# A hand-laid order of five instruction lists, laid out anew: Sinkhorn attention and a two-layer feed-forward block on one core

## The chip, the cores and the metric

The kernel runs on one NeuronCore of a Trainium2 chip. The core has a matrix engine (PE, TensorE), three engines for element-wise work (DVE, ACT and POOL), and a sequencer engine (SP) that here only issues transfers. Each engine works through its own list of instructions, strictly in order, and waits on semaphores for the others. Transfers are issued by POOL (loads from device memory that convert f32 to bf16) and by SP (transposing copies inside the on-chip memory, and the stores of the result).

The metric is the device time of one execution in microseconds: the median over several runs.

## What is computed

Four batches (B) with eight heads (H), 768 positions, 64 channels. The sequence is cut into eight blocks of 96. A learned 8x8 matrix per batch and head is made doubly stochastic by five rounds of Sinkhorn normalisation, and mixes the blocks of k and of v. Each block of q then attends to its own mixed block. The result, 3072 tokens of 512 channels, goes through a feed-forward block with a learned slope for negative values.

```python
for _ in range(5):
    P = np.exp(P - np.max(P, axis=-1, keepdims=True))
    P = P / (np.sum(P, axis=-1, keepdims=True) + 1e-09)
    P = P / (np.sum(P, axis=-2, keepdims=True) + 1e-09)
k_sorted = np.einsum('bhij,bhjcd->bhicd', P, k_b)
v_sorted = np.einsum('bhij,bhjcd->bhicd', P, v_b)
scores = scale * np.matmul(q_b, k_sb.transpose(0, 1, 2, 4, 3))
attn = softmax(scores)
x = np.matmul(attn, v_sb)          # then (B, S, H*D) -> 3072 x 512
h = x @ w_in                       # 512 -> 2048
g = np.maximum(h, 0.0) + alpha * np.minimum(h, 0.0)
out = g @ w_out                    # 2048 -> 512
```

## The kernel before

The kernel first builds a graph of 1190 steps. A step is a small function that issues one or some instructions, with the engines that may run it, the tiles it reads and writes, and so the steps it depends on (`_Graph.add`). A step that may run on two or three engines carries no fixed one (`EITHER`, `ANY`, `SMALL`).

The order is written out by hand in the constant `SEQ`: a list of step numbers. `arrange` walks through it and appends each step to the list of its engine. A letter behind a number (`p`, `a`, `d`) puts the step on POOL, ACT or DVE; without one it goes to the first engine that it may use. An entry such as `i15Y` isn't a step of the graph but 15 filler products: PE multiplies the identity with itself into the PSUM bank of that letter, and nobody reads the result (line 1047). `emit` then works out, for these five lists, the semaphore waits that are left. So the order of the steps on each engine, the engine of the free steps, and the number and place of the fillers follow from `SEQ` alone.

The work in stages, for one batch or for the whole:

- **Start.** PE runs a burst of 208 tiny products and then fillers, while q, k and v of batch 0 are loaded and the Sinkhorn rounds go back and forth between DVE and ACT. The result `Pb` is spread over the partitions by PE (step 79), and DVE makes the mixing matrix of it.
- **Preparation of a batch.** `prep_q` transposes q (steps 81, 83, 85, 87 for batch 0); `prep_k` and `prep_v` mix the blocks on PE, and ACT, DVE or POOL copy the result into KT and VS. For batches 1 to 3, `conv_k` and `conv_v` first spread k and v into sparse tiles (KSz, VDz), mostly on POOL, and q is loaded head by head (QN, eight loads per batch) and turned by six transposing copies that SP issues (`turn_q`). Each of these six reads all eight heads.
- **Attention of block g** (0 to 31). Scores on PE (line 756 for batches 1 to 3), row maxima on DVE (nf, line 765), Exp on ACT (Esb, line 793), a transposing copy by SP (ET, line 798), product with V on PE (line 813), reciprocal and scaling (rec, xq), and a transposition into xT, by PE or by SP. Blocks of batch 0 take a way without the transposing copies.
- **Feed-forward.** `ffn1` makes 128 hidden channels for two or four blocks of tokens (line 875), ACT and DVE apply the slope (lines 885 and 889), and `ffn2` sums over the hidden channels for 128 tokens in four parts (line 915); a copy and a store follow. These two carry most of the products and are laid between the attention steps.

The steps that are named below:

| Steps | What they are |
|---|---|
| 4, 5, 6 | loads of q, k, v of batch 0 |
| 126 to 129 | loads of the four parts of w_in; the hidden channels of the first half need 126 and 127 |
| 130, 131 | loads of the two halves of w_out; the first two parts of `ffn2` need 130, the last two 131 |
| 134; 143, 144 | loads of k, and of the two halves of v, of batch 1 |
| 135 to 142 | loads of the eight heads of q of batch 1 |
| 173 to 178 | the six transposing copies of q of batch 1 |
| 365, 366; 367 | loads of the two halves of v, and of k, of batch 2 |
| 44 | the first Exp of the Sinkhorn rounds |
| 39, 40, 9 | copies of the identity on ACT: selk, sel0 and identb |
| 151, 153, 162 | scaling of block 0, and the copies into xT of blocks 0 and 1 |
| 188 | the first `ffn1` |
| 252 to 255 | the four parts of the first `ffn2` |
| 382, 385, 386 | scores of block 8 (the first of batch 1), its transposing copy, its product with V |

Of the kernel before, what the change touches and what calls it, by code (L numbers as in the profile page):

```python
# [38 lines left out]
232 206 183 230 184 207 192 193 185d 198 209 142 199 186 i1Y 231 237 210 141 194 195 221 208 131 187 213 200  # L39
211 212 222 244 214 201 223 215 216 248 245 224 249 202d 246 247 203 204d 250 251 217 225 258 218 236 226 262  # L40
263 219 220 234 241 235 227d 266 267 259 260 173 228 229 252 238 276 268 239 253 264 242 269 305 172 288d 170
174 240 280 261 279 286 243 270 315 265 289 290 277 278 271 287 293 294 306 307 272d 273 308 275 291 274 281
292 297 295 342 282d 298 283 309 284 296 301 302 285 316 343 317 310 299 344 300 328 311d 303 304 312 314 313d
320 326 332 32 321d 345 346 327 169p 333 324 329 347 325 353 348d 254 171p 349 334 335 175 354 255 256 350d
323 367 318 395 330 382 331 396 319d 392 336 351 393 383 384 397 394 419 416 420 322 352d 355 356 358d 31 365
398 399 337 366 357 338 408 421 409 359 257 425 417 400 418 426 422 339 428 360d 361 427 423 424 411 449 410
385 340 368 446 429 362 363 439 450 451 455 430 364d 447 448 369 176 458 459 414 443 456 415 386 387 388d 412
452 453 370 454 440 389 401 460 371 438 390d 402 476 488 457 479 413 403 404d 489 405 372 512 177 469 431 406d
432 477 178 441 461 480 444 478 482 442 481 485 433 434d 490 524 491 373 483 472 435 378 377 486 374 436 487
513 380 445 462 375 484 509 463 510 464d 470 379 471 506 507 381 511 465 466d 508 525 514 376 521 522 523 518  # L50
519 520 515 516d 526 527 492 517 474 545 475d 542 168 554 560 391 493 543 546 544 547 468 500 501 494d 555 548
473 561 549 550 502 437 495 496d 562 407 503d 551 552 556 499 577 553 563 578 579 498 504 505 533 528 529 557
558 589 530d 535 534 538 539 571 572 590 583 584 580 341 531 581 625 626 537 536 569 582 586 591 540 587 585
622 570d 541 573 574 575 532 600 576 627 588 623 631 598 624 599 564 632 559 628 629 565 601 634 566d 567 635
602 592 630 603 633 568d 637 636 655 638 639 608 604 605 593 594 595d 610 649 650 640 652 596 653 656 657 609
597 641 642 651 654 664 665 666 661 662 663 606 667 607 658 611 659 687 688 612 668 613 643 684 696 685 660
669 689 686 697 690 691 676 677 682 711 467 680 702 693 694 703 704 683d 695 678 698 692 699 679 713 714 644
645 497 700 670 705 722 723 731 732 810 712 719 720 751 681 733 734 717 817 744 752 646d 812 715 721 724 671
672 725 745 816 718 766 673d 728 767 742 753 726 727 647 729 730 674 706 748 701 757 707 768 618 769 743d 754
708d 758 759 749 750 801 802 755 756 716 746 763 764 747 735 736 760 737d 761 803 765 740 709 762 741 621 789  # L60
777 790 783 784 619 776 786 787 778d 813 785 779 788 836 837 791 792 780 793 775 781 738 804 795 796 782d 811
798 799 797 838 615 814 815d 620 830 770 614 617 818 819 844 845 800 616 771 821 772d 864 831 846 848 874 839
820 648 822 824 823 773 827 805 806 825 794 849 826 832 833 828 807d 829 808 847 872 852 875 865 675 855 873d
834 853 835 850 883 851 854 866 840 841 867 710 876 842d 843 774 877 884 856 857 858 878 879 885 886 898 899
887 859 861 860 912 913 862 880 863 868 869 870d 900 889 924 944 881 882 890 892 891 893 895 925 945 896 894
914 906 926 907 897 908 909 950 910 911 871 946 901 951 927 918 919 920 921 922 923 952 902 903 904d 915 739
932 933 934 935 936 947 948 928 953 970 937 938 939 905 941 942 916d 981 917 982 971 972 943 961 940 958 809
959 973 996 929 1010 930d 931 954 962 997 998 983 960 964 965 963 967 968 1022 955 956d 966 984 969 957 949
# [1021 lines left out]
```

## Time and profile before

| What | us |
|---|---|
| Median of three runs | 235.51 (234.73 to 236.08) |
| The profiled execution, its own time | 235.32 |
| Its span, from the first to the last instruction | 233.6 |
| PE busy in the span | 225.4 |
| DVE, ACT, POOL busy | 167.6, 156.0, 102.7 |

The profile is that of one execution. The span leaves out what lies before the first and behind the last instruction, 1.7 us here. In the lines that follow, L875 is line 875 of the kernel; PE is the matrix engine's products and PEld its weight loads, which overlap them. A timeline line gives the start, the length, the engine, the line, the operation and what it writes and reads; in brackets stands how long the engine was idle before it, and what ended that. Products overlap, so the length of a line with several of them is the time from the first start to the last end. A stretch's line gives its length, the busy time of each engine with the number of its instructions, and behind them the granted clock of PE, the share of the transfer engines and the GB/s.

### The profile page before, as it was taken

Reading aid. Unit: us, or ns where it says so; the run is one execution under the profiler, and the core shown is the slowest. Engines: PE = TensorE matmul, PEld = TensorE weight load, DVE = VectorE, ACT = ScalarE, POOL = GpSimd, SP = SyncE. Lnnn points to the kernel's source line nnn. Section 1 sums busy time; section 2 is a strip of 40 time slices with the busy share of each in tenths; the row PEclk is TensorE's granted clock in tenths of the full one; section 3 lists DMA queues with packets and bytes.
Section 4 is the critical chain, followed back from the end, with each engine's and each line's share of the span. In section 5 each row is a group of like instructions: output and inputs, shape, how many; then the busy total and the mean of one; then the engine's idle time right before and its main releaser. Section 6 shows DMA issues by size and latency. Waiting matters only on the chain.

```text
span 233.6 us, 6277 instructions
## 1 busy us (share of the span) xinstructions
PE 225.4 (96%) x2528; PEld 140.4 (60%) x2556; DVE 167.6 (72%) x339; ACT 156.0 (67%) x417; POOL 102.7 (44%) x149
## 2 busy tenths in 40 slices
PE   6989999999999999999999999999999999999995
PEld 4356588795666666665566565555555555555653
DVE  5769799999878788586689668467787677544541
ACT  4187666989889678778888677766676674333431
POOL 7999139849049994863969953000000000000000
PEclk9999999999999999999999999999999999999999
DMA  5999999996996899869939997944643523410203
GB/s 66 220 206 204 218 200 185 186 182 99 218 189 106 115 152 174 196 102 225 192 63 164 137 103 164 154 90 79 130 107 74 112 51 109 124 45 0 94 0 135
DMA packets 73389, 31.36 MB, mean 134 GB/s; under 512 B 64512, under 2 KB 68368, under 8 KB 73360
## 3 DMA queue, kind: packets, MB, share of 16 engines
q0 software_dynamic: 24816, 13.63, 43.5%
q1 hardware_dynamic: 48544, 17.33, 37.2%
q8 instruction: 20, 0.33, 0.6%
q14 instruction: 9, 0.07, 0.1%
HBM read 27.28 MB, written 6.29 MB: 144 GB/s over the span
## 4 chain that ended last, share of the span: by engine, by line
PE 86%; DMA 4%; POOL 4%; DVE 3%; issue 2%; ACT 1%; POOLq 0%
PE psH L875 33%; PE psYP L915 28%; PE psYP L1047 4%; DMA VST<-in_v_dram 4%; PE psS L915 4%; PE psO L813 3%; PE psS L756 3%; POOL VDz L401 2%; PE psYP L668 2%; PE psYP L709 2%; PE psS L771 1%; PE psO L848 1%; DVE hT L401 1%; PE psS L781 1%; PE psO L915 1%
## 5 line engine op out<-in xcount | busy, mean ns | idle before, releaser
L889 DVE SCALAR_TENSOR_TENSOR hT<-t,omaT,psH 128x384 bf16<-128x384 f32 (+1 forms) x140 | 76.5, 568 | 37.4 <-ACT t L885 36.5
L875 PE MATMUL psH<-xT,w_in_bf 128*128 128x384 bf16 (+1 forms) x560 | 96.7, 310 | 0.6 <-DVE hT L889 0.6
L885 ACT ACTIVATE t<-psH 128x384 f32<-128x384 f32 x126 | 60.9, 493 | 44.5 <-PE psH L875 41.6
L915 PE MATMUL psYP<-w_out_bf,hT 128*128 128x512 bf16 x310 | 79.2, 379 | 1.4
L875 PEld LDWEIGHTS psH<-xT,w_in_bf 128*128 128x128 bf16 x560 | 50.0, 98 | 29.0 <-DVE hT L889 2.1
L915 PEld LDWEIGHTS psYP<-w_out_bf,hT 128*128 128x128 bf16 x336 | 30.8, 98 | 28.3 <-DVE hT L889 0.3
L793 ACT ACTIVATE Esb<-psS,nf 96x96 bf16<-96x96 f32 x192 | 46.1, 345 | 0.9 <-DVE nf L765 0.8
L401 POOL COPY VDz<-VST 64x384 bf16<-64x384 bf16 x40 | 34.5, 862 | 17.4 <-DMA VST<-in_v_dram 10.4
L655 POOL COPY KSz<-KS 64x512 bf16<-64x512 bf16 x36 | 22.0, 611 | 16.6 <-DMA KS<-in_k_dram 8.2
L765 DVE TENSOR_REDUCE nf<-psS 96x8 f32<-96x768 f32 x24 | 22.8, 950 | 6.4 <-PE psS L756 6.2
L826 DVE TENSOR_TENSOR xq<-psO,rec 96x512 bf16<-96x512 f32 x30 | 20.5, 684 | 0.7
L431 POOL DMA_DIRECT2D QN<-in_q_dram x24 | 19.9, 846 | 0.7 <-POOL QN L491 0.6
L401 ACT ACTIVATE outstg<-psYP 128x512 f32<-128x512 f32 x15 | 9.0, 601 | 7.7 <-PE psYP L915 7.5
L813 PEld LDWEIGHTS psO<-VS,ET 112*128 112x128 bf16 x248 | 11.1, 98 | 4.0 <-ACT xT L401 0.2
L1047 PE MATMUL psYP<-identb 128*128 128x512 bf16 x39 | 12.7, 470 | 0.8 <-ACT identb L401 0.8
L813 PE MATMUL psO<-VS,ET 112*128 112x65 bf16 x248 | 12.7, 194 | 0.0
L756 PEld LDWEIGHTS psS<-KT,QTz 128*128 128x128 bf16 (+1 forms) x192 | 10.7, 101 | 3.2 <-ACT KT L401 0.2
L401 ACT ACTIVATE VS<-psYP 112x512 bf16<-112x512 f32 x16 | 11.0, 688 | 2.1 <-PE psYP L714 1.1
L756 PE MATMUL psS<-KT,QTz 128*128 128x96 bf16 (+1 forms) x192 | 12.2, 207 | 0.0
L709 PEld LDWEIGHTS psYP<-BDV,VDz 128*128 128x128 bf16 x192 | 8.3, 98 | 3.0 <-POOL VDz L401 0.3
L401 ACT ACTIVATE KT<-psYP 128x512 bf16<-128x512 f32 x14 | 8.4, 600 | 2.2 <-PE psYP L668 2.0
L709 PE MATMUL psYP<-BDV,VDz 128*128 128x64 bf16 x192 | 9.5, 193 | 0.1
(140 smaller groups left out, 200.2 us busy)
## 6 DMA issues: line engine op xcount, KB each, us to landing
out_dram<-outstg SPq DMA_DIRECT2D x23, 256.0 KB, 2.5
KS<-in_k_dram POOLq DMA_DIRECT2D x3, 768.0 KB, 10.1
QN<-in_q_dram POOLq DMA_DIRECT2D x24, 96.0 KB, 4.5
w_in_bf<-in_moe_w_in_dram POOLq DMA_DIRECT2D x4, 512.0 KB, 16.8
w_out_bf<-in_moe_w_out_dram POOLq DMA_DIRECT2D x2, 1024.0 KB, 18.7
VST<-in_v_dram POOLq DMA_DIRECT2D x4, 384.0 KB, 11.1
hT<-in_q_dram POOLq DMA_DIRECT2D x1, 768.0 KB, 7.4
VST<-in_v_dram POOLq DMA_DIRECT2D x1, 768.0 KB, 12.8
```

Of the source, the lines that this page charges most:

```text
L401: return e.activation(o, i, ACTF.Copy) if e is nc.scalar else e.tensor_copy(o, i)
L655: G.add(POOL, lambda e, hp=hp: e.tensor_copy(AP(KSz, hp * 64 * 3072 + u % 3 * 1024 + hp * 64, [[3072, 64], [128, 8], [1, 64]]), AP(KS[n], ...
L709: inst = e.matmul(AP(t, off + dd * 64, [[row, 128], [1, 64]]), AP(VDz, (u % VSL * 8 + dd) * 128, [[VSL * 1024, 128], [1, 128]]), AP(BDV, b ...
L756: inst = e.matmul(o, AP(QTz[n], hp * 3072 + h4 * 768 + i * 96, [[6144, 128], [1, w]]), AP(KT[n], (h4 * 8 + i) * bk, [[ld, 128], [64, 2], [ ...
L765: G.add(DVE, lambda e: e.tensor_reduce(AP(nx, 0, [[8, 96], [4, 2], [1, 4]]), AP(psX, 0, [[1024, 96], [512, 2], [96, 4], [1, 96]]), AxisLis ...
L793: inst = e.activation(AP(Esb[me], p * 128, [[1024, 96], [64, 2], [1, 48]]), AP(psX, (p // 4) * 512 + (p % 4) * 96, [[1024, 96], [48, 2], [ ...
L813: inst = e.matmul(AP(psZ, hp * 512 + h4 * 68, [[1024, 128], [1, 65]]), AP(ET[me] if far else ET[m], pos(h4, hp) * 96, [[800, nk], [1, 128] ...
L875: inst = e.matmul(AP(pt, poff + x * n, [[1024, 128], [1, n]]), AP(w_in_bf, kt * DFF + (ft + x) * 128, [[KT_TILES * DFF, 128], [1, 128]]), ...
L885: G.add(ACT, lambda e: e.activation(AP(t1[tb], 0, [[384, 128], [1, k * n]]), AP(pt, poff, [[1024, 128], [1, k * n]]), ACTF.Relu, scale=-1. ...
L889: G.add(DVE, lambda e, x=x: e.scalar_tensor_tensor(out=AP(hT, (ft + x) * RING + tok % RING, [[FT_TILES * RING, 128], [1, n]]), in0=AP(t1[t ...
L915: inst = e.matmul(AP(bank[0], bank[1], [[1024, 128], [1, n]]), AP(hT, ft * RING + tok % RING, [[FT_TILES * RING, 128], [1, 128]]), AP(w_ou ...
L1047: inst = e.matmul(AP(t, off, [[1024, 128], [1, 512]]), identb[:, :], AP(identb, 0, [[128, 128], [0, 4], [1, 128]]))
```

## The change

Only `SEQ` is replaced. The graph and its 1190 steps, `arrange`, `emit` and all tiles are as before. In the excerpt the lists run up to the first steps of batch 1; all the rest of `SEQ` is laid out anew in the same way.

```diff
 SEQ = """
-0 2 11 7 3 10 4 1 8 25 39 42 43 5 9 27 44 17 33 i1Y 45 i4Y 24 46 47 6 48 49 14 50 28 i2Y 51 52 53 i15Y 23 54
-55 143 56 57 58 26 59 127 60 61 62 21 63 64 126 65 66 22 67 128 68 69 29 70 71 16 72 73 13 74 129 85 86 87 75
-76 77 78 40 79 80 81 37 88 134 82 96 97d 94 91 92 98 38 89 130 12 144 95 90d i2Y 140 93a 83 84 100 i3Y 99d 20
-136 101d 102d 105a 103d 154 i3Y 104 106 155 109 114 115 15 145 146 110 111 107d 112 113 i3Y 116 117d 147 108a
-118 119d 148 122 123d 137 120 156 121 124 139 132 19 125d 135 233 133 157 i2Y 158 159 149 150 160d i3G 179 180
-i1P 41 138 i2P 161 162d 151 152 18 181 30 35 36 34 153d 163 188 182 196 164 165 205 166 167p 197 189 190 191
...
+0 7 11 16 2 10 3 1 4 21 42 43 8 44 9 30 45 40 46 i3O 5 47 48 25 49 33 50 13 37 51 i15O 52 53 54 55 6 56 57 28
+127 58 29 59 60 14 61 62 63 64 65 12 66 67 68 27 69 134 70 71 34 126 72 87 73 83 74 88 128 35 85 41 17 75 76
+i4P 38 129 77 84 78 23 81 39 144 79 80 82 19 96 143 86 89 98 90d 99 97d 91 94 92 i4P 95d 93 100 102 105a 101d
+103a 104d 26 154 145 130 155 107a 110 114 112 111d 106 113 156 115d 109a 108 146 116 137 120 117d 118 147 119
+121d 24 139 157 122 124 132 123 125d 20 232 148 133 i1O 158 236 i3O 159 160d 136 149 18 150 179 151d 231 161
...
 """.split()
```

What follows from the new list, engine by engine:

- **Fillers.** Before, 42 in thirteen groups: 1, 4, 2 and 15 ahead of the first transposition of q, the rest in groups of 1 to 3, the last of them between the first products of `ffn1`. After, 30 in six groups: 3 and 15 ahead of the first transposition of q, then 4, 4, 1 and 3; the last group stands ahead of the product with V of block 0. All fillers, before and after, stand ahead of step 382 on PE.
- **POOL's queue of loads.** Before: 4, 5, 6, 143, 127, 126, 128, 129, 134, 130, 144, then the heads 140, 136, 137, 139, 135, 138, 142, 141, then 131; later 367, 365, 366. After: 4, 5, 6, 127, 134, 126, 128, 129, 144, 143, 130, then the heads 137, 139, 136, 141, 135, then 131, then the heads 142, 140, 138, then 366; later 365 and 367.
- **SP.** Before, the six transposing copies of q of batch 1 were mixed with those of the attention blocks 8 to 10 and a store. After, all six stand ahead of the first one of an attention block, in the order 173, 174, 178, 176, 175, 177. The last four stores are the same, in the same order.
- **ACT and DVE.** 56 steps change their engine: 23 from ACT to DVE, 23 from DVE to ACT, four from POOL to DVE, three from DVE to POOL, two from ACT to POOL, one from POOL to ACT. At the start, ACT runs the first Exp (44) ahead of 9 and 40, and 39 later between two copies of q; DVE runs the masks and memsets 33, 27, 35, 41 and 17 between steps of the Sinkhorn rounds. The scaling of block 0 (151) moves from ACT to DVE, the copies 153 and 162 from DVE to ACT.
- **PE.** The products themselves are the same; the order is laid out anew over its whole length. Its last seven steps are the same, in the same order.

More of the change, by code (lines that the diff above doesn't have):

```diff
@@ L43 @@
[L43 to L47, printed above, removed]
@@ L78 @@
-1176d 1171 1177 1178 1179 1180 1181 1182 1183
+0 7 11 16 2 10 3 1 4 21 42 43 8 44 9 30 45 40 46 i3O 5 47 48 25 49 33 50 13 37 51 i15O 52 53 54 55 6 56 57 28
[3 more added lines that the diff above has]
+121d 24 139 157 122 124 132 123 125d 20 232 148 133 i1O 158 236 i3O 159 160d 136 149 18 150 179 151d 231 161
@@ L79 @@
+1183
 """.split()
```

74 lines of the change are left out of this document (40 added, 34 removed).

## The prediction

> **What bounds the kernel now.** The page gives PE as busy for 96% of the span, so I went straight to the busy times of a few stretches of my choice.
>
> ```profile
> 0.00:11.40 11.40, 9.63 (x230) 4.56 (x230) 7.23 (x38) 3.38 (x9) 10.06 (x21) 1.00 0.85 140
> 11.40:29.10 17.70, 16.18 (x406) 10.90 (x405) 13.85 (x30) 12.99 (x27) 12.41 (x16) 1.00 1.09 210
> 29.10:54.80 25.70, 25.57 (x417) 20.90 (x414) 24.59 (x61) 20.50 (x37) 16.96 (x28) 1.00 1.41 177
> 54.80:69.00 14.20, 13.39 (x136) 8.37 (x136) 11.43 (x17) 12.48 (x38) 5.84 (x9) 1.00 1.03 185
> 69.00:230.60 161.60, 160.34 (x1354) 95.64 (x1374) 110.48 (x196) 106.29 (x307) 57.46 (x78) 1.00 0.68 114
> ```
>
> Columns: length, then the busy time of PE, weight loads, DVE, ACT and POOL. A busy PE may be a PE with little in it, so I asked for the weight loads of the last long stretch by form, and took each product's spacing from the chain that ended last.
>
> ```profile
> L875 PEld LDWEIGHTS psH<-xT,w_in_bf 128*128 128x128 bf16 x412 | 38.1, 98 | 26.1 <-DVE hT L889 1.4
> L915 PEld LDWEIGHTS psYP<-w_out_bf,hT 128*128 128x128 bf16 x296 | 27.1, 98 | 25.1 <-DVE hT L889 0.3
> ```
> ```profile
> 222.25 1.73 PE psS L915 x8
> 223.98 1.30 PE psH L875 x8
> ```
>
> A product of 384 columns takes 1.30/8 = 0.163 us, one of 512 takes 1.73/8 = 0.216 us. From 69.0 to 230.6 us the 412 + 296 products of these two rows alone fill 67.0 + 63.9 = 131 of 161.6 us; 666 other weight loads (1374 - 708) share 31 us, 46 ns each. Nothing waits there. **So the last 160 us are PE work that no order shortens**; an order can gain, or lose, before 69 us, and it can break a stretch that now runs without a gap. Before 69 us stand the filler products, the start, and one dense stretch.
>
> ```profile
> 3.66 7.82 PE L1047 MATMUL psYP<-identb 128*128 128x512 bf16 x22 [0.76 <-ACT identb L401]
> 13.13 0.36 PE L569 MATMUL psYP<-Pb,sel 32*128 32x8 bf16 x8 [0.86 <-ACT sel L401]
> 17.61 0.35 PE L759 MATMUL psH<-KT,QTz 64*128 64x96 bf16 x8 [0.17 <-ACT QTz L401]
> 29.11 0.83 PE L875 MATMUL psH<-xT,w_in_bf 128*128 128x192 bf16 x8
> 54.81 0.50 PE L756 MATMUL psS<-KT,QTz 128*128 128x96 bf16 x8
> 57.63 1.47 PE L875 MATMUL psH<-xT,w_in_bf 128*128 128x384 bf16 x8 [0.57 <-DVE hT L889]
> ```
>
> The first row is 22 of the 42 fillers; 29.11 is the first ffn1 (op 188), 54.81 the first score of batch 1 (op 382). Those are my two milestones, because in both orders the work ahead of each is the same apart from the fillers.
>
> **The change, part by part.**
>
> *Fillers.* 12 fewer at 0.216 us is 2.6 us of PE work, all of it ahead of op 382. If every other wait stayed, the time would fall by 2.6 us. But a filler stands where PE has nothing to do, so the question is what is late once it is gone.
>
> *Start to the first ffn1.* The rows:
>
> ```profile
> 2.92 0.28 DVE L506 TENSOR_REDUCE mkj<-identf 128x8 f32<-128x128 f32 x1
> 12.07 0.21 DVE L562 TENSOR_TENSOR Pb<-P,cs 32x64 bf16<-32x64 f32 x1
> 24.18 0.69 DVE L401 CAST VS<-psO 112x512 bf16<-112x512 f32 x1 [0.46 <-PE psO L714]
> 25.83 0.64 DVE L826 TENSOR_TENSOR xq<-psYP,rec 96x512 bf16<-96x512 f32 x1
> ```
> ```profile
> 3.51 0.24 ACT L551 ACTIVATE P<-P 32x64 f32<-32x64 f32 x1
> 25.94 1.72 ACT L832 ACTIVATE xq<-psO,rec 96x64 bf16<-96x64 f32 x8 [1.33 <-DVE rec L821]
> ```
>
> The first Exp of the Sinkhorn chain (3.51) goes ahead of selk and identb on ACT; what it reads is ready at 2.92, where mkj begins right behind it: 0.6 us won. Five small DVE jobs (three masks, two memsets) move into that chain where no Exp covers them; the row of mkj bounds each at 0.28, so up to 1.4 and at least 0.3, and I take 0.8, three masks. Pb stands at 12.5 instead of 12.29. The selector that made PE wait 0.86 us is copied early now. On PE 18 fillers end four warm ones (0.86 us) sooner, at about 10.5; then come three transposes of q at 0.3, four fillers, one transpose: 12.6. The spread goes from 13.13 to about 12.6: 0.5 won. It is partly lost: ACT now copies two q transposes after selk, so the last K tile is written at about 17.3, and the first score comes at 17.4 instead of 17.61. Then DVE has two row maxima (0.95, by the row of L765 below) and five V tiles (0.69) in a row: 5.4 us from about 18.2, with 0.3 of waits V is complete at 23.9 against 24.87 (24.18 + 0.69). After that come the product with V (0.4 with its latency), two reciprocals and two scalings on DVE, 1.8 together now that block 0 is scaled by DVE (0.64) and no longer by ACT (1.72), the maxima of block 2 (0.95) and its 16 products and hand-overs (1.1), which stand ahead of op 188 on PE: the first ffn1 falls at **28.2 instead of 29.1: 0.9 won**, between 0.3 and 2.0: the low end if the four later groups of fillers (4, 4, 1 and 3) hold PE while its data is there, the high end if they never do. Moved SP steps don't reach this stage: SP has nothing to issue between the two first loads and the turning of q at 45 us.
>
> *The loads.* Here I see the price. Big loads go through POOL's queue one after another, in the order of issue. Each row is a DMA view of a short window: size and time from issue to landing; above them its issue on POOL.
>
> ```profile
> 12.32 0.94 POOL L965 DMA_DIRECT2D w_out_bf<-in_moe_w_out_dram  x1
> ```
> ```profile
> w_out_bf<-in_moe_w_out_dram POOLq DMA_DIRECT2D x1, 1024.0 KB, 26.0
> KS<-in_k_dram POOLq DMA_DIRECT2D x1, 768.0 KB, 21.0
> w_in_bf<-in_moe_w_in_dram POOLq DMA_DIRECT2D x1, 512.0 KB, 18.0
> ```
> ```profile
> 38.35 0.82 POOL L431 DMA_DIRECT2D QN<-in_q_dram  x1
> 39.16 0.89 POOL L965 DMA_DIRECT2D w_out_bf<-in_moe_w_out_dram  x1
> ```
> ```profile
> w_out_bf<-in_moe_w_out_dram POOLq DMA_DIRECT2D x1, 1024.0 KB, 11.4
> QN<-in_q_dram POOLq DMA_DIRECT2D x1, 96.0 KB, 6.5
> ```
> The other issues, of POOL and of SP, are from the timeline:
>
> ```profile
> 11.07 0.73 POOL L960 DMA_DIRECT2D w_in_bf<-in_moe_w_in_dram  x1
> 11.76 0.61 POOL L449 DMA_DIRECT2D KS<-in_k_dram  x1
> 44.86 6.47 SPq L439 DMA_TRANSPOSE QTz<-QN  x3
> ```
> ```profile
> 67.11 1.31 SPq L439 DMA_TRANSPOSE QTz<-QN  x1
> ```
> The next two rows are the landing times of the first of these transposes alone, and of all 18.
>
> ```profile
> DMA to landing us min/median/max: 6.6/6.6/6.6
> DMA to landing us min/median/max: 3.1/3.6/8.1
> ```
>
> Landings before: last w_in 29.1 (11.07 + 18.0), K of batch 1 at 32.8, first half of w_out 38.3, last q head 44.85, second half of w_out 50.6. So K takes 3.7 us, a half of w_out 5.6, half of a V load about 1.8, a q head (44.85 - 38.3 - 1.8)/8 = 0.6. The queue is full throughout, so the last of the lot lands at 50.5 in either order. In the new order K of batch 1 goes ahead of three w_in parts and half of V behind them: w_in is whole at 31.0, while the ffn1 that needs it stands at about 32: hidden, with 1 us of cover. The first half of w_out lands at 40.1 (V's half is ahead of it), ffn2 asks for it at 28.2 + 11.9 = 40.1: even. But **three q heads (142, 140, 138) now stand behind the second half of w_out**: it lands at 48.7, 1.9 sooner, and the last q head at 50.5, 5.7 us later than before. The transposes of q wait for all eight heads, so the first is issued at 50.5, not 44.86. Its duration then is between 3.1 and 8.1 us; before, it shared the engines with w_out for 6.6. I take the median 3.6, as only half a V load (1.8 us) is behind it in the queue: landing 54.1. PE itself would reach op 382 at 28.2 + 25.7 (the old distance) - 0.2 for the one filler that stood in between = 53.7. So **op 382 starts at 54.2, against 54.81: 0.6 won of 2.6**, between 53.2 and 55.2. On SP all six turnings now stand ahead of the first transpose of E (op 385): six issues of 1.3 us end at 58.4, where E of block 8 is ready at about 57.6; 0.8 us of delay that is hidden, as its product comes 11 us of PE work after op 382.
>
> *After op 382* the old order loses time once, the 0.57 us before 57.63, and about as much in smaller pieces (54.8 to 69.0: 0.81 idle). The other loads of batch 2 are spread now (half of V early, K after it), the copy jobs that PE waited for are ahead while PE waits for q: 0.4 won, between 0 and 1. The 56 copies that change engine cancel (23 from ACT to DVE, 23 back). From 69 us on I count 0: the distance in PE work from a score to its product with V, counted in products at the spacings above, shrinks from 9.2 to 7.6 us at the shortest. The step needs about 6 by the rows below (0.95 + 8 x 0.24 + 3.0 to land, 0.2 between them).
>
> ```profile
> L793 ACT ACTIVATE Esb<-psS,nf 96x96 bf16<-96x96 f32 x192 | 46.1, 345 | 0.9 <-DVE nf L765 0.8
> L765 DVE TENSOR_REDUCE nf<-psS 96x8 f32<-96x768 f32 x24 | 22.8, 950 | 6.4 <-PE psS L756 6.2
> ET<-Esb SPq DMA_TRANSPOSE x24, 3.0
> ```
>
> The tail is unchanged: its last seven PE steps and its last four stores stand in the same order.
>
> **Sum**: 0.6 + 0.4 = 1.0 off the profiled execution's 235.32 (span 233.6) gives 234.3. That execution lies 0.2 under the median of 235.51; I predict **234.4** for the median. Bounds: on the median's scale the best ends (1.6 + 1.0) give 232.9, the worst (-0.4 + 0) 235.9.
>
> **The rivals.**
> *All fillers saved*: q is turned in time, or PE is late anyway. For it: the DVE is 24.59 of 25.70 busy up to op 382, so PE may lose less than the loads say. Against: eight heads wait in a queue with no gap. It gives 235.51 - 2.6 = 232.9.
> *Nothing left*: op 382 stays at 54.8 or a little over, and some step after 69 us waits; 235.2 to 236.2.
> *Slower*: the first transposes of q collide with V of batch 2 as they did with w_out. At the 6.6 us of before they land at 57.1, at 8.1 at 58.6; op 382 then starts 2.3 to 3.8 us later than before, less the 0.4 won after it. It decides from a landing at about 56.4 (54.8 + 1.2 + 0.4). Against it: that load is less than half the size. It gives 237.4, up to 238.9.
> *The clock falls back.* Two rows of the fillers alone:
>
> ```profile
> 6.15:9.45 3.30, 3.30 (x9) 1.21 (x8) 1.00 1.26 222
> 9.45:11.20 1.75, 1.75 (x9) 0.69 (x7) 1.00 1.08 224
> ```
>
> Until about 9.5 us eight products take 3.30 us (0.41 each), after it seven take 1.75 (0.25 with a cut one at each end, 0.216 in full): a half clock first. If 12 fewer fillers let PE fall back once for as long as one such stretch of 3.3 us, half of it is lost: about 1.7, or 236.1 and more. The Trainium skill, "TensorE: Matmul & The Clock Gate", Part 1, says that the array starts at half clock and is released after a busy window of about 3.4 us, and throttled again after an idle one, with windows that run freely. The trace agrees with the release (5.8 us after the first filler); no row shows a fall back, and PE has no idle stretch near that length in the new order by my count.
>
> **How the numbers follow.** Forecast (233.6 to 235.2) 0.45; all saved 0.20; nothing left 0.20; collision 0.12; clock 0.03. A measurement of this kernel tells about 0.5% (1.2 us) from no change, so faster means under 234.3, slower over 236.7. The forecast's range straddles 234.3: half of it and the first rival make 0.43 faster; the other half and "nothing left" 0.43 within; the rest 0.14 slower. The range holds the forecast, "all saved" with the 0.6 us of small gaps after 54.8 won as well (232.3), "nothing left", and reaches to 236.8, short of the collision's 237.4: it leaves out 0.15, and a little below.
>
> **What would show it.** First ffn1 near 28.2; last q head landing near 50.5 and the first q transpose issued right then; PE idle before op 382 with the transpose as releaser, for some tenths of a us; no idle over 0.5 us from 69 us to the end. I am wrong if the q heads land by 47, if op 382 starts before 53 or after 56, or if gaps appear in the last 160 us.

## The result, and the profile after

The new order is **slower by 1.2%**: 238.41 us (median of seven, 237.24 to 249.6) against 235.01 us for the kernel before (median of seven, 234.57 to 236.08); the ratio is 1.0116, with an interval from 1.0083 to 1.0148. Three of the seven executions took 241.8 to 249.6 us, at a mean granted clock of 0.984 to 0.991; ratios, here and below, leave out executions that took over 1.5% more than the fastest of their kernel, medians do not. The prediction said 234.4 and a range up to 236.8: the change went the other way. The profiled execution took 238.41 us, its span is 236.6 (before 235.32 and 233.6), so 3.0 us have to be found.

The stretches of the prediction, cut in the same places, in the kernel after (length, then busy time of PE, weight loads, DVE, ACT and POOL):

```profile
11.40:29.10 17.70, 14.66 (x389) 11.08 (x388) 13.37 (x28) 12.64 (x22) 14.31 (x23) 1.00 1.08 209
29.10:54.80 25.70, 23.95 (x386) 19.09 (x383) 22.31 (x55) 20.18 (x37) 16.38 (x25) 1.00 1.32 177
54.80:69.00 14.20, 12.63 (x131) 7.69 (x132) 10.80 (x17) 10.53 (x36) 7.23 (x11) 1.00 1.09 158
```

PE is busy for 1.5 us less than before in the first stretch, where most of the missing fillers were, and 1.6 us less in the second, where only one is missing: there, and in the third with 0.8 us less, PE stands idle. Its timeline gives the places (start, length, operation; in brackets the idle time before it and its releaser). An op is a step of the graph, as in the prediction.

```profile
26.99 1.49 PE L875 MATMUL psH<-xT,w_in_bf 128*128 128x192 bf16 x16
...
40.91 1.04 PE L915 MATMUL psYP<-w_out_bf,hT 128*128 128x512 bf16 x4 [0.43 <-DMA w_out_bf<-in_moe_w_out_dram]
...
49.17 1.04 PE L915 MATMUL psYP<-w_out_bf,hT 128*128 128x512 bf16 x4 [0.77 <-DMA w_out_bf<-in_moe_w_out_dram]
...
54.85 0.51 PE L756 MATMUL psS<-KT,QTz 128*128 128x96 bf16 x8 [0.21 <-DMA QTz<-QN]
...
64.98 0.50 PE L756 MATMUL psS<-KT,QTz 128*128 128x96 bf16 x8 [1.51 <-DMA QTz<-QN]
...
72.81 0.41 PE L813 MATMUL psO<-VS,ET 112*128 112x65 bf16 x8 [0.66 <-DMA ET<-Esb]
```

The first row is op 188: 26.99 against 29.11, **2.1 us ahead**. The fourth is op 382: 54.85 against 54.81. The whole lead is gone there, 1.4 us of it in the three waits that the rows show. The last two are op 428 (scores of block 10) and op 402 (product with V of block 9): here the new order falls **behind**. Before, neither of them waited:

```profile
63.63 0.50 PE L756 MATMUL psS<-KT,QTz 128*128 128x96 bf16 x8
...
72.04 0.41 PE L813 MATMUL psO<-VS,ET 112*128 112x65 bf16 x8
```

The groups of PE from 54.8 us to the end show the same for all 24 blocks of batches 1 to 3; first the two rows of before, then those of after (behind the bar the mean of one, then the idle time ahead of the group and its releaser):

```profile
L756 PE MATMUL psS<-KT,QTz 128*128 128x96 bf16 (+1 forms) x192 | 12.2, 207 | 0.0
L813 PE MATMUL psO<-VS,ET 112*128 112x65 bf16 x192 | 9.8, 194 | 0.0
```
```profile
L756 PE MATMUL psS<-KT,QTz 128*128 128x96 bf16 (+1 forms) x192 | 12.2, 207 | 1.8 <-DMA QTz<-QN 1.7
L813 PE MATMUL psO<-VS,ET 112*128 112x65 bf16 x192 | 9.8, 194 | 1.1 <-DMA ET<-Esb 1.1
```

Waits for transposing copies: 0.0 us before, 2.8 us after, and 0.2 of that is the wait ahead of op 382 itself. From op 382 to the end of the span it is 233.6 - 54.81 = 178.8 us before and 236.6 - 54.85 = 181.8 after. So the 3.0 us are lost behind op 382, and nothing is left of the early start. The waits for copies that SP issues make 2.6 us there, while the kernel before loses only the 0.57 us to DVE that the prediction shows at 57.63. That places 2.1 of the 3.0 us; the other 0.9 is in no single wait that the profile lists. The chain of waits says it too (the page's shares of the span by what ended last, before and after):

```profile
PE 86%; DMA 4%; POOL 4%; DVE 3%; issue 2%; ACT 1%; POOLq 0%
```
```profile
PE 66%; DMA 18%; POOL 9%; issue 4%; ACT 1%; DVE 1%; SPq 0%; POOLq 0%
```

**Why these copies are late.** SP's timeline of the kernel after, and the DMA view at two moments: while the copy 175 is being issued (57.6 us), and from 64.4 us, where 367 and 401 are issued, and the queues from 67 to 70 us, while the load and the copy are both under way (q0 is POOL's queue, q1 is SP's: packets, MB, share of 16 engines):

```profile
51.46 11.23 SPq L439 DMA_TRANSPOSE QTz<-QN  x6
62.74 7.86 SPq L798 DMA_TRANSPOSE ET<-Esb  x3
```
```profile
QTz<-QN SPq DMA_TRANSPOSE x1, 7.9
```
```profile
KS<-in_k_dram POOLq DMA_DIRECT2D x1, 768.0 KB, 7.4
ET<-Esb SPq DMA_TRANSPOSE x1, 8.3
```
```profile
q0 software_dynamic: 86, 0.53, 93.0%
q1 hardware_dynamic: 85, 0.02, 5.5%
```

The first two turnings landed 3.4 us after their issue, at 54.81 and 56.25. Then half of V of batch 2 (365) was issued at 54.84, and the next three turnings, issued from 54.23 on, took 6.7, 6.9 and 7.9 us. Op 428 needs 175, which the new order issues fifth: it landed at 64.84, and PE asked 1.5 us sooner. The load had landed at 61.41; 175 came 3.4 us behind it, after the two copies that SP had issued ahead of it (60.90 and 62.46). ET of block 9 (401), issued at 64.34, met K of batch 2 (367), issued at 64.47: it landed at 72.67, behind K at 71.82.

The queue rows show how. From 67 to 70 us the two queues moved the same number of packets, 86 and 85. A packet of the load has 6 KB in the mean (0.53 MB in 86), one of the copy 0.25 KB (0.02 MB in 85). So the copy moved some 20 KB in 3 us, while the whole copy (96 x 1024 bf16, 196 KB) takes 2.9 us alone (below): nearly all of it has to wait until the load's big packets are through. The Trainium skill, "DMA: Bandwidth & Descriptors", "Queues, rings and completion order", says that each transfer engine takes turns between its queues packet by packet; the rows agree, 86 packets to 85.

### The profile page after: what moved, and what is told of

It is laid out like the page before. It is cut to its first block, busy times and chain, and to the rows that moved or that the text cites. A ratio compares the mean times of both kernels' runs of the same rounds, so it can differ in the third digit from the quotient of the medians.

```text
span 236.6 us, 6269 instructions
## 1 busy us (share of the span) xinstructions
PE 224.4 (95%) x2544; PEld 139.3 (59%) x2544; DVE 166.5 (70%) x340; ACT 152.6 (64%) x409; POOL 101.4 (43%) x149
## 4 chain that ended last, share of the span: by engine, by line
PE 66%; DMA 18%; POOL 9%; issue 4%; ACT 1%; DVE 1%; SPq 0%; POOLq 0%
PE psH L875 28%; PE psYP L915 26%; DMA ET<-Esb 6%; DMA VST<-in_v_dram 5%; DMA QN<-in_q_dram 4%; PE psS L915 4%; PE psS L756 3%; DMA QTz<-QN 3%; POOL KSz L655 3%; PE psO L813 2%; PE psYP L709 2%; POOL QN L431 2%; POOL hT L401 1%; POOL QN L491 1%; PE psYP L668 1%
## 5 line engine op out<-in xcount | busy, mean ns | idle before, releaser
L885 ACT ACTIVATE t<-psH 128x384 f32<-128x384 f32 x126 | 60.8, 492 | 53.5 <-PE psH L875 52.9
L915 PE MATMUL psYP<-w_out_bf,hT 128*128 128x512 bf16 x336 | 84.4, 380 | 1.2 <-DMA w_out_bf<-in_moe_w_out_dram 1.2
L401 POOL COPY VDz<-VST 64x384 bf16<-64x384 bf16 x40 | 33.7, 843 | 18.7 <-PE psYP L709 8.7
L826 DVE TENSOR_TENSOR xq<-psO,rec 96x512 bf16<-96x512 f32 x31 | 21.1, 681 | 0.4
L821 DVE RECIPROCAL rec<-psO 96x8 f32<-96x8 f32 x31 | 6.2, 199 | 7.9 <-PE psO L813 7.8
L401 ACT ACTIVATE outstg<-psYP 128x512 f32<-128x512 f32 x13 | 7.8, 603 | 4.5 <-PE psYP L915 4.5
L401 ACT ACTIVATE VS<-psYP 112x512 bf16<-112x512 f32 x14 | 9.6, 686 | 0.7 <-PE psYP L709 0.5
L915 PE MATMUL psS<-w_out_bf,hT 128*128 128x512 bf16 (+1 forms) x48 | 9.6, 344 | 0.0
```

The source lines that it names most:

```text
L401: return e.activation(o, i, ACTF.Copy) if e is nc.scalar else e.tensor_copy(o, i)
L885: G.add(ACT, lambda e: e.activation(AP(t1[tb], 0, [[384, 128], [1, k * n]]), AP(pt, poff, [[1024, 128], [1, k * n]]), ACTF.Relu, scale=-1. ...
L915: inst = e.matmul(AP(bank[0], bank[1], [[1024, 128], [1, n]]), AP(hT, ft * RING + tok % RING, [[FT_TILES * RING, 128], [1, 128]]), AP(w_ou ...
```

## The experiments

Theory: the loss is where a transposing copy with little room meets a load. Rivals: the new order of products is the loss by itself; or the smaller number of fillers. All kernels are made by moving entries of `SEQ` or adding fillers; the same products run in all of them, but for fillers. Ratios are against the kernel before, measured in the same round, with the interval.

| Run | Median us | Ratio (interval) |
|---|---|---|
| after | 238.41 | 1.0116 (1.0083 to 1.0148) |
| turns_in_order | 239.87 | 1.0174 (1.0106 to 1.0242) |
| k2_later | 243.46 | 1.0365 (1.0332 to 1.0398) |
| order_and_k2 | 238.27 | 1.0116 (1.0093 to 1.0139) |
| heads_first | 237.37 | 1.0110 (1.0077 to 1.0143) |
| batch2_early | 245.34 | 1.0422 (1.0386 to 1.0457) |
| old_heads_late | 235.88 | 1.0025 (1.0012 to 1.0037) |
| old_start_new_rest | 247.64 | 1.0438 (1.0409 to 1.0466) |
| old_turns_and_loads | 238.33 | 1.0098 (1.0056 to 1.0139) |
| old_transfers | 236.22 | 1.0041 (1.0013 to 1.0069) |
| fillers_back | 242.06 | 1.0280 (1.0252 to 1.0308) |
| fillers_at_16 | 239.73 | 1.0195 (1.0167 to 1.0222) |
| new_start_old_rest | 234.28 | 0.9960 (0.9942 to 0.9978) |
| new_start_filled | 234.38 | 0.9971 (0.9950 to 0.9992) |
| new_start_v2_first | 234.57 | 0.9973 (0.9954 to 0.9992) |
| new_start_both | 234.46 | 0.9977 (0.9954 to 0.9999) |

### One collision removed at a time

```diff
 turns_in_order, SP:
-173 174 178 176 175 177
+173 174 175 176 177 178
```

> The kernel after, with the six transposing copies of q of batch 1 on SP in the order 173, 174, 175, 176, 177, 178 instead of 173, 174, 178, 176, 175, 177; nothing else moves. Theory (the scores of block 10, op 428, wait because the copy they need is issued fifth): the copy 175 takes the third place, is issued near 54.2 and lands near 60.9, as the third copy did; op 428 is asked for at 63.4 and waits no more: 1.5 us come off at 65 us. What is left of it at the end depends on ET of block 9 (op 402 waited 0.7 to 0.9 us for it): if that lands as late as before, nearly all is lost again at 72.8 us and the time is 238.0 to 238.4; if it moves along, 236.9. Rival (the transfers as a whole are late, whatever their order): the wait moves to another score and the time stays at 238.4 with an idle stretch of 1.5 us before 66 us.

```profile
54.06 0.51 PE L756 MATMUL psS<-KT,QTz 128*128 128x96 bf16 x8 [0.34 <-DMA QTz<-QN]
72.22 0.41 PE L813 MATMUL psO<-VS,ET 112*128 112x65 bf16 x8 [2.54 <-DMA ET<-Esb]
```

The wait of op 428 is gone, as the theory said: 175 went third and landed at 60.38. But PE only came sooner to op 402, whose ET (63.76 to 72.08) still landed behind K of batch 2 (71.09). Its wait grew from 0.66 to 2.54 us. A wait was moved, not removed, and the time is no better (238.0 to 238.4 was expected for this case; the median came out at 239.87).

```diff
 k2_later, POOL:
-... 410 367 408 438 411 381 413 442 468 412 380 ...
+... 410 408 438 411 381 413 442 468 367 412 380 ...
```

> The kernel after, with the load of K of batch 2 (367) issued on POOL about 8 us later, behind a step of 72 us instead of at 64.5 us. Theory (ET of block 9, op 401, took 8.3 us because it ran beside that load): it lands near 68 to 69 us, 4 to 5 us after its issue, and op 402 waits no more: 0.7 us off, 237.7; the wait of op 428 (1.5 us) stays. Rival (401 is slow because of the copies ahead of it on SP, not of the load): it lands at 72.7 as before and the time stays at 238.4.

The DMA view while ET of block 9 is issued, the one while ET of block 11 is issued, then the timeline and two stretches:

```profile
ET<-Esb SPq DMA_TRANSPOSE x1, 2.9
```
```profile
KS<-in_k_dram POOLq DMA_DIRECT2D x1, 768.0 KB, 7.9
ET<-Esb SPq DMA_TRANSPOSE x1, 9.2
```
```profile
82.34 0.60 PE L813 MATMUL psO<-VS,ET 112*128 112x65 bf16 x8 [3.85 <-DMA ET<-Esb]
```
```profile
78.40:82.30 3.90, 0.09 (x1) 0.00 (x0) 0.66 (x2) 0.00 (x0) 3.84 (x6) 1.00 1.93 124
82.30:85.60 3.30, 3.26 (x24) 2.03 (x25) 1.89 (x4) 0.49 (x1) 3.13 (x5) 0.50 1.45 252
```

The mechanism is shown: without the load, the very same copy took 2.9 instead of 8.3 us. The prediction of the time failed: K now met ET of block 11, which has less room, and PE stood for 3.85 us. Behind that the granted clock was 0.50 for 3.3 us, which by my estimate costs another 1.6 us (half of it).

```diff
 order_and_k2: the order of turns_in_order on SP, and on POOL
-... 410 367 408 438 411 381 ...
+... 410 408 438 411 367 381 ...
```

> The kernel after, with the six turnings in the order 173 to 178, as in the first experiment, and K of batch 2 (367) issued some 3 us later, behind step 411 on POOL. Theory (a copy that is under way or queued beside a load lands about with that load; the loss at 65 and 72 us is the copy 175 and ET of block 9, each beside one load): ET of block 9 runs alone and lands 3 to 4 us after its issue at 63.8; that of block 10 runs beside K and lands near 74, up to 0.5 us late; both waits are gone or small and the time is 236.2 to 237.2. Rival (the new order leaves no room anywhere, so one freed wait is always lost at the next copy): 238 or more, with another idle stretch of over 1.5 us between 65 and 85 us.

```profile
59.76 0.50 PE L756 MATMUL psS<-KT,QTz 128*128 128x96 bf16 x8 [1.35 <-DMA QTz<-QN]
77.57 0.40 PE L813 MATMUL psO<-VS,ET 112*128 112x65 bf16 x8 [1.93 <-DMA ET<-Esb]
```

ET of block 9 ran alone in 3.0 us, but that of block 10 met K and landed at 77.43, where I had it near 74; and the second turning, issued at 53.06, met the half of V and landed at 59.62. The rival was right as far as single moves go: three placings of K, three late copies.

### The q heads, and all of batch 2 early

```diff
 heads_first, POOL:
-... 135 131 142 ... 22 ... 140 ... 138 ...
+... 135 142 140 22 138 131 ...
 and on PE:
-... 254 316 312 332 346 328 320 349 255 324 395 ...
+... 316 312 332 346 328 320 349 324 254 255 395 ...
 batch2_early: the same, SP in the order 173 to 178, and on POOL
+... 131 366 365 367 ...
```

> The kernel after, with the q heads 142, 140 and 138 (and the memset 22 that 138 needs) ahead of the second half of w_out (131) in POOL's queue, and parts 2 and 3 of the first ffn2 (254, 255), which need that half, laid behind the V products 316 to 324 on PE. Theory (the q heads behind w_out set the time of all six turnings): the last head lands near 46, the first turning is issued there and lands near 52.5, beside w_out; the turning that op 428 needs lands by 58; op 382 starts near 53.9, op 428 without a wait; some 2.5 us off, 235.9. Rival (no slack elsewhere: w_out, V of batch 2 and the turnings only push each other): w_out lands at 51 or later, the V loads later too, and as much is lost in new waits; 238 or more.

> The kernel after, with the q heads 142, 140, 138 ahead of the second half of w_out (131), the loads of batch 2 (366, 365, 367) right behind it in POOL's queue, the six turnings in the order 173 to 178, and parts 2 and 3 of the first ffn2 (254, 255) behind the V products on PE. Theory (a transposing copy is slow, 6 to 10 us, while a big load runs, 3 us alone; what counts is which copy runs beside a load): the queue is empty by 59 us, all turnings run beside loads and land between 53 and 62 us, mostly ahead of their scores, and the copies of E from block 8 on run alone in 3 to 4 us, so the wait of 0.7 to 2.5 us at 72 us is gone: 235 to 236. Rival (the turnings beside the loads are so slow that op 382 or 396 waits): 237 or more, with an idle stretch ahead of a score between 54 and 62 us.

With the heads first nothing was gained, 1.0110 where 235.9 us was hoped for; 175 stood fifth and K beside ET of block 9, as in the kernel after. Only the times of this run are used. The other run is the clearest failure. The DMA view at the issue of the first turning, PE's timeline, and the stretch behind it:

```profile
QTz<-QN SPq DMA_TRANSPOSE x1, 17.5
```
```profile
63.18 0.82 PE L756 MATMUL psS<-KT,QTz 128*128 128x96 bf16 x8 [5.09 <-DMA QTz<-QN]
```
```profile
63.20:69.00 5.80, 5.80 (x30) 3.15 (x31) 3.40 (x5) 2.42 (x9) 0.00 (x0) 0.50 0.96 191
```

A copy issued at 45.67, beside a queue that held w_out, V and K, landed at 63.13, just behind the last of them (62.43). I had bounded a copy beside loads at 10 us. **It has no such bound: here it landed with the last load that was queued beside it.** The granted clock was 0.50 all through the 5.8 us behind that wait, a loss of about 2.9 us by my estimate (half of them). The table sets copies beside the load that they met, if any (173 and 178 are turnings; 385, 401, 431 and 461 are ET of blocks 8 to 11):

| Run, copy | Issue | Landing | Load beside it, landing |
|---|---|---|---|
| before, 173 | 44.86 | 51.51 | w_out 50.57 |
| before, 385 | 58.91 | 67.56 | V 66.79 |
| after, 178 | 54.23 | 60.90 | V 61.41 |
| after, 401 | 64.34 | 72.67 | K 71.82 |
| k2_later, 401 | 64.54 | 67.45 | none |
| k2_later, 461 | 73.03 | 82.20 | K 80.40 |
| order_and_k2, 401 | 65.67 | 68.64 | none |
| order_and_k2, 431 | 68.86 | 77.43 | K 75.45, q head 77.97 |
| batch2_early, 173 | 45.67 | 63.13 | K 62.43 |

It is not a law. The copies that SP had queued behind another one came later, as 175 in the kernel after (3.4 us behind V); and two turnings landed well ahead of the last load, 174 in `order_and_k2` (59.62, V at 61.98) and 175 in `old_turns_and_loads` (63.92, K at 67.70).

### The old transfers with the new products, and the reverse

```diff
 old_heads_late (from the kernel before), POOL:
+... 141 131 142 140 138 ...     (140, 138 and 142 stood ahead of 141)
 old_start_new_rest: all lists as before up to op 382, from there as after
 old_turns_and_loads (from the kernel after), SP and POOL:
-173 174 178 176 175 177 385 401 431 341 461
+173 174 175 385 176 401 177 431 178 341 461
-... 365 409 357 31 410 367 ...
+... 365 367 409 357 31 410 ...     (and 381 goes ahead of 380)
 old_transfers: the same, and the edits of heads_first
```

> The kernel before, with one part of the change alone: the q heads 142, 140 and 138 behind the second half of w_out (131) in POOL's queue. Theory (the late q heads cost little by themselves; it is the copy 175 in the fifth place and K of batch 2 beside ET of block 9 that cost): the last head lands near 50.6, the first turning near 54, beside no load; op 382 starts at 54.6 to 55.2 and op 428 (asked at 63.4) has its copies by 62; 235.0 to 235.8. Rival (the late heads are the cause): op 382 or 428 waits 1 us or more, 236.5 to 238.

> All five lists as in the kernel before up to the first scores of batch 1 (op 382), and from there as in the kernel after; 42 fillers. The turnings of q and K of batch 2 (367) are then as early as before, V of batch 2 follows at once. Theory (the loss behind op 382 comes from turnings and ET copies beside loads, that is from the late q heads and the late loads of batch 2, which stand ahead of op 382 or near it): the waits at 65 and 72 us are under 0.5 us each and the time is 234.8 to 235.8. Rival (the new order behind 382 loses by itself, since it leaves less room between a copy and its product): an idle stretch of 1 us or more between 60 and 75 us, 236.5 to 238.

> The kernel after, with the list of SP around the turnings as in the kernel before (173, 174, 175, then 176, 177 and 178 each behind an ET copy, of blocks 8, 9 and 10), and K of batch 2 (367) right behind its V (365), so that no big load runs later than about 66 us; the q head 381 of batch 2 goes behind step 439, as it needs 178. Theory (the loss behind op 382 is the meeting of turnings and ET copies with loads that come singly, not the new order of products): the copy 175 lands by 62, ET of blocks 8 and 9 by 67 to 69, both waits are gone and no new one over 0.5 us follows up to 100 us: 235.8 to 236.8. Rival (the new order of products leaves too little room for any placing of the transfers): 237.6 or more, with an idle stretch of over 1 us between 60 and 85 us.

> As the run old_turns_and_loads, and besides the q heads 142, 140 and 138 (with the memset 22) ahead of the second half of w_out (131), as before the change, and parts 2 and 3 of the first ffn2 (254, 255) behind the V products 316 to 324 on PE. Theory (transfers again, now from the q heads on): the turnings start near 46 and land between 52 and 57 beside w_out; op 382 starts near 53.9 without a wait; 235.0 to 236.0. Rival (the new order of products itself loses): 237 or more.

`old_heads_late` takes the one part of the change that the prediction made most of, and puts it into the old order: 0.25% slower, 235.88 us, a little over the 235.0 to 235.8 expected. So late q heads by themselves cost about 0.6 us. Its profile lists no wait of PE for a turning, but 0.94 us at 47.2 and 0.50 us at 69.8 us for steps of POOL.

`old_start_new_rest` was to be near 235 and came out at 247.64. Its profiled execution is the longest of four (251.13 us), so the size of this wait is not that of the others:

```profile
72.70 0.61 PE L709 MATMUL psYP<-BDV,VDz 128*128 128x64 bf16 x8 [6.45 <-POOL VDz L401]
```

Where the two orders are joined, K, V and V of batch 2 are issued in one row with a turning beside them (177: issued 54.62, landed 71.08), and POOL waits for the last half. So the run can't tell the new order of products from its transfers; the joint makes a collision of its own, as in `batch2_early`.

The last two answer the question. With SP's list and K of batch 2 put back, the waits at 65 and 72 us shrink to one of 0.68 us; later ones appear (0.70 at 154.6 and 1.12 at 186 us), and the ratio, 1.0098, can't be told from that of the kernel after. Its executions differ more than others: 236.3 and 236.4, in the range that the theory gave, but also 238.3, 238.8 (the profiled one) and 242.3. With the q heads put back too, the view of waits lists none for PE from 54.8 to 150 us. The timeline of `old_transfers` at op 382, its stretch from there, and its first wait:

```profile
55.42 0.50 PE L756 MATMUL psS<-KT,QTz 128*128 128x96 bf16 x8
```
```profile
54.80:69.00 14.20, 14.09 (x149) 9.00 (x150) 11.05 (x18) 12.04 (x37) 7.49 (x10) 1.00 0.97 161
```
```profile
153.35 0.51 PE L756 MATMUL psS<-KT,QTz 128*128 128x96 bf16 x8 [0.47 <-DMA QTz<-QN]
```

From op 382 to the end of the span (234.1) it is 178.7 us: 178.8 before, 181.8 after. Without the waits that the profiles list there (0.57 before, 2.63 after, 0.47 here) it is 178.2, 179.2 and 178.2. By these profiles **the new order of products costs nothing behind op 382; the order of its transfers costs nearly all of the 3 us.** How much of it each of the edits gives back isn't separated: `heads_first` and `old_turns_and_loads` each hold one part of them, and neither is enough.

What is left against the kernel before is 0.4%, or 1.0 us between the profiled executions (236.29 and 235.32). Op 382 comes 0.6 us later (55.42 against 54.81); in this execution the clock was at half from about 19 to 22.5 us. And 0.5 us lies outside the span: 2.2 us of each execution, against 1.7 before. `heads_first` and `batch2_early`, which share the edits of the q heads and of ops 254 and 255, show 2.1 to 2.2 us too; why stays open.

### Fillers

```diff
 fillers_back:
+... 15 i12H 188 ...
 fillers_at_16:
+... i3Y 154 ... i4Y 110 ...
```

> The kernel after, with 12 fillers more, 2.6 us of PE work, right ahead of the first ffn1 (op 188), so 42 in all as before the change. Theory (the lead of 2.2 us at op 188 is lost again in waits for w_out and for the turnings of q): op 188 starts at 29.5, the waits ahead of ops 252, 254 and 382 (1.4 us) and part of that ahead of 428 go instead, and the end moves by 0 to 0.8 us: 238.4 to 239.2. Rival (PE work sets the end, and the transfers only follow it): the end moves by all of the 2.6 us: 241.0.

> The kernel after, with 7 fillers more between 15.8 and 18.1 us, where PE has two idle places of 0.8 and 0.9 us: 3 ahead of the first scores of block 1 (154) and 4 ahead of the first V product (110). From 15 to 19 us PE is busy for 2.3 of 4 us in the kernel after and for 3.8 of 4 in the kernel before; in the profile of the kernel with the q heads first the granted clock was 0.50 to 0.79 from 19 to 24 us, right behind that stretch. Theory (the sparse stretch lets the clock fall back in some executions, and that is what lies behind the times over 241): no execution over 240, the others at 237.3 to 238.4 as before, since the fillers stand where PE is idle. Rival (the high times have another cause): 2 or 3 of 7 executions still over 241.

`fillers_back` took 2.8 us of span more than the kernel after (239.4 against 236.6; by the ratios it is 1.6%, or 3.9 us), at least what the rival said. So the missing fillers are not what was lost. The way there is another than the rival's, though. Op 188 moved by 2.4 us (to 29.43), op 382 by 0.9 (to 55.75) and op 402 by 0.4 (to 73.21), so up to here the loads did swallow it, as the theory had it. Then new waits came:

```profile
102.25 0.40 PE L813 MATMUL psO<-VS,ET 112*128 112x65 bf16 x8 [1.01 <-DMA ET<-Esb]
...
158.26 0.51 PE L756 MATMUL psS<-KT,QTz 128*128 128x96 bf16 x8 [1.88 <-DMA QTz<-QN]
```

The second one is the order of the turnings again: for batch 3 the new list issues the second turning (675) last but one of six, while blocks 25 and 26 need it. The first one is open: its copy took 4.8 us, 3.0 in the kernel after, though POOL issued no load between 84 and 100 us. So in the order after, a shift of under 1 us at ops 382 and 402 was followed by waits for copies that have no room.

`fillers_at_16` did not bring the clock back in all executions (0.984, 0.991 and 0.993 in three of six), and its ratio is worse than that of the kernel after. Why 7 products in idle places cost that is open. Its profiled execution, the longest of the six (242.56 us), waits for the same kinds of copies as the kernel after does, but for longer: 1.70 us at 66.0, 2.21 at 75.4 and 2.42 at 159.6.

### What is worth keeping

```diff
 new_start_old_rest: all lists as after up to op 188, from there as before; on POOL
-... 129 144 143 130 ...
+... 129 130 144 143 ...
 new_start_filled: besides, i3Y ahead of 154 and i4Y ahead of 110
 new_start_v2_first: new_start_old_rest with 367 behind 365 and 366
 new_start_both: both
```

> All five lists as in the kernel after up to the first ffn1 (op 188), and from there as in the kernel before; the first half of w_out (130) goes ahead of V of batch 1 (143, 144), as the old order asks for it early; 31 fillers. Theory (the new start is worth 2.2 us at op 188, and the loss comes from the order behind it): no collision as at 64 and 72 us in the kernel after; the lead is lost in part because the second half of w_out and the turnings of q are no earlier than before: op 382 starts at 53.6 to 54.4 and the time is 234.0 to 235.0. Rival (the lead at op 188 is worthless, since the loads set the time): 235.0 to 236.0.

> The kernel with the new start and the old rest, with 7 fillers more in PE's idle places between 15.8 and 18.1 us (3 ahead of step 154, 4 ahead of step 110). In the profile of that kernel without them the granted clock was 0.50 to 0.70 from 19.3 to 22.7 us, in others of its executions 1.0. Theory (the sparse stretch from 15 to 19 us lets the clock fall back in some executions): the mean granted clock is 0.999 or 1.0 in all executions and the times lie at 233.4 to 234.0. Rival (the fall back has another cause, as the mean clocks of 0.984 to 0.993 in three executions of the filled kernel after suggest): the clock is again under 0.995 in a third of them, 234.0 to 235.0.

> The kernel with the new start and the old rest, with K of batch 2 (367) behind the two halves of V of batch 2 (365, 366) in POOL's queue instead of ahead of them. PE waited 0.84 us at 68.8 us for a step on POOL that reads the half landing at 66.8. Theory (that half lands 3 to 4 us sooner then, and K, asked for at 88 us, has room): the wait goes and 0.6 to 0.9 us come off, 233.0 to 233.6. Rival (the same bytes run in the same stretch, and a turning or an ET copy that lands with the last load is late instead): 234.0 to 234.6.

> The new start and the old rest, with both edits of the last two runs: 7 fillers more between 15.8 and 18.1 us, and K of batch 2 behind its V. If their gains add: 233.4 to 234.0. If both only remove waits that come back at the next transfer: 234.3 to 234.7, as each of them alone.

All four beat both kernels: 0.2 to 0.4% faster than before, and they cannot be told from each other. Their start is the new one, and SP's list is the old one. The edit of `new_start_v2_first` removed the wait it aimed at (0.84 us at 68.8 us), without a gain that shows; nor does the one of `new_start_filled` show any in the time. In the profiles of the last three, op 188 starts at 27.2 us, 1.9 ahead of the kernel before, and op 382 at 53.5 to 54.1, 0.7 to 1.3 ahead. So with the order of SP's copies left alone, 0.5 to 0.9 us (0.2 to 0.4% of 235) of the lead at op 188 reach the end.

## Why the prediction was wrong

- **Start: mechanism right, size too small.** Op 188 was put at 28.2 and came at 26.99. The gain of the start was sized at 0.9 and measured 2.1, just past the bound of 2.0. The stretch of two row maxima and five V tiles on DVE took 5.7 us (17.27 to 22.97), as summed, but it began 0.9 us sooner than the 18.2 that I gave: Pb stood at 11.99 instead of 12.5, and the first score came at 16.73 instead of 17.4. The next row is the first filler behind the V products: it waits for ACT's last copy of V and starts at 22.90, where I had V complete at 23.9.

```profile
22.90 0.39 PE L1047 MATMUL psO<-identb 128*128 128x512 bf16 x1 [0.52 <-ACT VS L401]
```

- **Loads: right.** The first half of w_out landed at 40.87 (predicted 40.1) and PE waited for it 0.43 us; the last q head landed at 51.44 (50.5), and the first turning was issued at 51.46, right then. Its copy took 3.4 us (3.6). PE waited 0.21 us ahead of op 382, "some tenths". Op 382 came at 54.85, in its range of 53.2 to 55.2, though 0.65 us past the value: the two halves of w_out cost 0.43 and 0.77 us, where I had the first as even and saw the second only as landing sooner.
- **The step that failed** is "After op 382 ... 0.4 won, between 0 and 1", with "From 69 us on I count 0". Behind op 382 3.0 us were lost, and PE waits there 2.6 us for transposing copies, where it waited for none before. I followed the first of the six turnings to its score and counted the five others as time on SP ("six issues of 1.3 us end at 58.4", "0.8 us of delay that is hidden"). The last was issued at 61.38, and the score that mattered was that of block 10, whose copy 175 the diff puts fifth; its place in the list and the place of 365 were both in front of me. For E I took 3.0 us a copy, the median over the kernel, and compared it with a room of 7.6 us; but the room has to hold the copy *beside the load that the new order puts there*, 8.3 us at 64 us.
- **The rival "slower"** had the right kind, a turning beside V of batch 2, at the wrong copy: the first one ran alone in 3.4 us, the third to fifth did not. Its time, 237.4 to 238.9, held the result, but by luck: it came from 2.3 to 3.8 us lost ahead of op 382, and op 382 was not late. With a chance of 0.12 it was rated low, as I weighed the one copy on my path and not the number of copies that could meet a load.
- **The clock** was given 0.03. It didn't fall in the profiled execution, but the mean clock of three of seven shows that it can; what starts it there is open.

## What to carry to other kernels

Follow every transfer that is moved to the step that reads it, not only the first, and set its duration by what runs beside it *in the new order*: alone 3 us, beside a load until about the landing of that load. Whether loads come bunched or spread doesn't decide it: the kernel before issues three loads of batch 2 from 54.1 to 57.5 us and no score or product waits for a copy, while `batch2_early` and `old_start_new_rest` bunch them beside a turning that is needed soon, and lose 4%. What counts is which copy stands beside a load, and how soon it is read. And a wait that is taken away is worth something only if the next transfer has room too: look at the next two before counting the gain.

## What the runs showed of the hardware that was not expected

- A transposing copy of E took 2.9 to 3.0 us alone and 8.3 to 9.2 us beside one load of 768 KB; one of q took 17.5 us beside a queue of several. In the table they land between 0.5 us ahead of and 2.0 us behind the load. Beside K of batch 2, from 67 to 70 us, the two queues moved packets one for one (86 and 85), though those of the load were some 25 times the size.
- The granted clock fell to 0.50 behind a wait of PE of 3.85 us, for 3.3 us. The Trainium skill, "TensorE: Matmul & The Clock Gate", Part 1, says that the array goes back to half clock after an idle window of about 3.4 us; that case agrees. In two others the clock fell without so long an idle stretch. In the profile of `order_and_k2` it was at half from 78.7 us, behind the wait of 1.93 us at 77.57; PE was busy for 1.48 of 3.40 us there. In the profile of `new_start_old_rest` it was at half from 19.3 to 22.6 us, and PE had no idle stretch over 0.84 us before it.

```profile
74.90:78.30 3.40, 1.48 (x16) 0.69 (x15) 1.44 (x5) 2.39 (x10) 2.62 (x4) 1.00 1.48 207
78.70:82.10 3.40, 3.40 (x20) 1.63 (x16) 2.33 (x5) 0.94 (x2) 3.13 (x4) 0.50 1.76 206
```
```profile
15.00:19.00 4.00, 2.51 (x84) 1.71 (x82) 3.17 (x6) 2.31 (x4) 2.51 (x4) 1.00 1.09 202
19.30:22.60 3.30, 3.30 (x78) 2.85 (x72) 2.73 (x5) 2.29 (x4) 3.24 (x6) 0.51 1.01 200
```

PE is busy for 3.83 us of the same 4 us before the change, so a sparse stretch may be enough. But it isn't always: in the profile of the kernel after, PE is busy for 2.33 of these 4 us, and the clock stayed at 1.00. The runs don't settle it: with the old rest, the mean clock was under 0.995 in 4 of 22 executions without the 7 fillers, in 2 of 24 with them, and in 14 of 77 of the kernel before.
